# RWKV-6 attention with a hypermixer behind it on one core: both chunks' queries on partition halves, paired mix products, one exp for the chunk decays, and a new split of the copies

## The chip, the core and the metric

The kernel runs on one core of a Trainium2 chip. The metric is device time in microseconds (us). The time before is a median of 3 runs. The profile is of one further execution, taken by the hardware profiler. Engines are named as in the profile: PE (matrix products), ACT (ScalarE), DVE (VectorE), POOL (GpSimd) and SP, which only issues loads here.

## What is computed

The first part is a linear attention with a decay for each channel, over 4 batches, 8 heads, 768 steps and 48 channels a head. The second part mixes the steps of a batch with a matrix that is made from the first part's output x.

```python
for t in range(S):                                   # attention, state is D x D per head
    cur = np.einsum('bhd,bhe->bhde', u[None] * kt, vt)
    y[:, :, t] = np.einsum('bhd,bhde->bhe', rt, state + cur)
    state = wt[:, :, :, None] * state + np.einsum('bhd,bhe->bhde', kt, vt)
...
wq = x @ w_q                                         # hypermixer, x is [B, S, 384]
wk = x @ w_k
W_tok = scale * np.einsum('bsd,btd->bst', wq, wk)
mixed = np.einsum('bst,btd->bsd', W_tok, x)
return (np.maximum(mixed, 0.0) @ w_out).astype(np.float32)
```

## The kernel before

**Tiles.** A tile `n` is 256 steps of one batch, all 8 heads: 12 tiles, 3 for each batch `b`. Each tile holds two chunks of 128 steps, and a chunk lies on one half of the 128 partitions, with two steps on each partition. The steps run on different engines and are pipelined over about three tiles.

For one tile, in order: `load` brings w, k, r and v (SP issues the four transfers, into three buffers for each); `log` (ACT) takes the logarithm of w; `sums` (PE) makes its running sums in three PSUM tiles `cw0` to `cw2`, and in spare columns of `cw2` the sum over each chunk; `expk` and `expr` (ACT) turn them into the factors for k (`em`) and r (in place); `decay` (ACT) makes the decay of each chunk, `pt`, in two exps over 48 partitions each, since two heads lie one above the other with a gap; `rdec` (DVE) and `kdec` (POOL) multiply into `RdS` and `KdS`; `trR` (PE) transposes both into `psT` and `evT` (DVE) copies that to `RKT`; `amat` (PE) makes two halves of the score matrix `A` and `mask` (DVE) masks them into `AmB`; `uk1`, `uk2` (POOL), `red` (DVE) and `vd` (POOL) make the diagonal term; `vcast` (ACT) casts v; `state` and `stadd` (PE) build the chunk state `Sn`, `stev` (DVE) scales it by `pt` into `SB`; `ymat`, `yst`, `yd` (PE) sum the output `Y`, and `yev` copies it to `X`, on ACT or DVE by the table `XA`.

Then the mixer's share of the tile: `xtr` (PE) transposes X, `xev` (ACT) copies that to `XT`, `qkmat` (PE) makes wk and the transposed wq of the tile, and `qkev` (ACT) copies them in two instructions to `wk_s` and `wqT`. When all three tiles of a batch are there: `tmat` (PE) sums wk^T X over the six chunks into `Tps` (64 rows), `tev` copies it (ACT), `mix` (PE) makes six pieces of 384 columns, `mixev` (ACT) applies the maximum with 0, `fin` (PE) multiplies by w_out, `finev` copies to `osb` (ACT or DVE by the table `FE`), and `store` issues two transfers from ACT's queue.

**What sets the order.** Every engine runs its instructions strictly in the order in which the program gives them. That order is written by hand: the lists `steps`, `first`, `last`, `bsteps`, `blast` give each step a time relative to its tile or batch, `start`, `bstart`, `lstart` place the tiles, batches and loads, and all steps are sorted by the sum. The times serve as sort keys alone. PSUM is shared by two groups of buffers: two large ones, through which `psT`, the two `A`, `Sn` and `Y` pass in turn, and four of one bank (`cw0` to `cw2`, `xt_ps`, `qk`, `Tps`, `mps`, `fps`). A transfer counts on one of eight completion semaphores (DMAHW0 to 7, loads and stores alike), and waits until the transfer before it on that semaphore has landed.

Lines that the prediction speaks of: all matmuls are issued in L60; `decay` L177, X L330 (ACT) and L332 (DVE), `XT` L347, qk copies L367 and L368, `mixT` L393, `osb` L410 (ACT) and L412 (DVE), stores L417, loads L138.

Of the kernel before, what the change touches and what calls it, by code (L numbers as in the profile page):

```python
# [25 lines left out]
def kernel(  # L26
# [17 lines left out]
    XA = (0, 1, 4, 5, 7, 8, 10, 11, )  # L44
    FE = (0, 1, 1, 1, 1, 1, 0, 1, 1, 1, 1, 1, 0, 1, 0, 1, 0, 0, 0, 1, 0, 0, 0, 0)
# [29 lines left out]
    Q2 = consts.tile([C, 2], BF16, tag="Q2")  # L75
# [70 lines left out]
    def sums(n):  # L146
# [3 lines left out]
        for i, m0, m1 in ((1, BI, BS), (2, BI, BI), (0, BS, BS)):  # L150
# [122 lines left out]
    def stadd(n, q):  # L273
        T["stadd", n, q] = True
        b, m = divmod(n, NU)
        if 2 * m + q:
            SB = T["SB", b, 2 * m + q]
            mm(T["Sn", n][:, q, 0:DM], ID128, SB, start=False)

    def stev(n, q):  # L280
# [6 lines left out]
            _rep(T["pt", n][:, q], 2, D), ALU.mult)  # L287
# [32 lines left out]
    def yev(n):  # L320
# [23 lines left out]
    def xev(n):  # L344
        T["xev", n] = True
        b, m = divmod(n, NU)
        nc.scalar.copy(T["XT", b][:, :, ds(m * C2, C2)], T["tp", n])  # L347

    def qkmat(n):
# [3 lines left out]
        qk = mtile([128, 3, 2, DH], F32, "qk")  # L353
        for cc in range(2):
            for kt in range(NK):
                mm(qk[:, 0, cc], XT[:, kt, ds((2 * m + cc) * C, C)], wk_sb[:, kt],
                   start=(cc == 0 and kt == 0), stop=(kt == NK - 1))
        for kt in range(NK):
            mm(qk[0:DH, 1:3].rearrange("p a c h -> p (a c h)"), T["wq"][:, kt],
               XT[:, kt, ds(m * C2, C2)], start=False, stop=(kt == NK - 1))  # L360
        T["qk", n] = qk

    def qkev(n):
        T["qkev", n] = True
# [25 lines left out]
    def mixev(b, i):  # L390
        T["mixev", b, i] = True
        n, dt = divmod(i, NK)
        nc.scalar.activation(T["mixT", b][:, dt, ds(n * 384, 384)], T["mps", b, i],  # L393
                             ACT.Relu)
# [9 lines left out]
    def finev(b, c):  # L404
# [4 lines left out]
        if FE[b * NCH + c]:  # L409
            nc.scalar.copy(osb, T["fps", b, c])  # L410
        else:
            nc.vector.tensor_copy(osb, T["fps", b, c])  # L412
# [40 lines left out]
    for i in range(NB):  # L453
# [4 lines left out]
        nc.vector.memset(PT[i], 0.0)  # L458
# [9 lines left out]
    def wcast():  # L468
# [26 lines left out]
        (10.87, mask, (1, )),
        (11.75, state, ()),
        (12.04, stadd, (0, )),
        (12.07, stev, (0, )),
        (13.75, stadd, (1, )),
        (13.78, stev, (1, )),  # L500
        (14.31, ymat, ()),
        (14.34, yst, ()),
        (14.34, yd, ()),
        (14.37, yev, ()),
        (16.62, xtr, ()),
        (16.65, xev, ()),
        (19.39, qkmat, ()),
        (20.61, qkev, ()),
    ]
    first = [  # L510
        (-8.58, log, ()),
        (-5.99, sums, ()),
        (-1.73, expk, ()),
        (-1.72, expr, ()),
        (1.28, uk1, ()),
        (1.84, decay, ()),
        (2.87, rdec, ()),
        (4.73, trR, (0, )),
        (5.68, kdec, ()),
        (5.83, trR, (1, )),  # L520
        (5.86, evT, ()),
        (5.9, uk2, ()),
        (7.74, vcast, ()),
        (8.69, amat, (1, )),
        (9.57, amat, (0, )),
        (9.6, mask, (0, )),
        (11.89, mask, (1, )),
        (11.99, state, ()),
        (13.95, red, ()),
        (14.96, ymat, ()),  # L530
        (15.18, stadd, (0, )),
        (15.21, stev, (0, )),
        (15.57, vd, ()),
        (16.02, yd, ()),
        (16.21, stadd, (1, )),
        (16.36, stev, (1, )),
        (16.63, yst, ()),
        (16.66, yev, ()),
        (17.25, xtr, ()),
        (17.45, xev, ()),  # L540
        (20.49, qkmat, ()),
        (20.85, qkev, ()),
    ]
# [145 lines left out]
```

## Time and profile before

| | |
|---|---|
| median of 3 runs | 130.83 us (129.42 to 132.07) |
| the profiled execution | 130.25 us, its span in the profile 128.4 us |
| busy PE, DVE, ACT, POOL | 102.0, 86.6, 88.4, 85.0 us of the span |
| granted TensorE clock, mean | 0.968 of full speed |
| moved by DMA | 24.83 MB, mean 193 GB/s |

A profile row gives a start or a group, then busy time, engine, line, operation and the tiles that it writes and reads (out<-in). "[1.20 <-DVE AmB]" behind a row means that the engine stood idle 1.20 us before it, until DVE's instruction on AmB was done. The chain that ended last is followed back from the last instruction, at each step to whatever released it. PE's matmuls overlap one another: each row's time runs from the first start to the last modelled end.

### The profile page before, as it was taken

The numbers are of one execution on the slowest core, as the hardware profiler recorded it, in microseconds if no ns is written. First come the engines' busy times: TensorE is split into PE (matmuls) and PEld (weight loads), VectorE is DVE, ScalarE is ACT, GpSimd is POOL, SyncE is SP. The second block draws the span as 40 slices with busy tenths as digits, with TensorE's granted clock in tenths as the row PEclk, the third lists the DMA queues.
The fourth block names the chain that finished last, engine by engine and source line by source line (L and its number), as shares of the span: only waits on it lengthen the run. The fifth ranks groups of instructions, "written<-read, shape, count | busy, mean of one in ns | idle before, by whom it ended". The sixth has DMA issues, their size and how long they took to land.

```text
span 128.4 us, 4125 instructions
## 1 busy us (share of the span) xinstructions
PE 102.0 (79%) x1732; PEld 66.6 (52%) x1732; DVE 86.6 (67%) x134; ACT 88.4 (69%) x185; POOL 85.0 (66%) x81
## 2 busy tenths in 40 slices
PE   0076839779794999989999989799999899986900
PEld 0025437465572765645757655467566665652500
DVE  6003599788779759966959798569778979340330
ACT  3066683998885466799889686999896738456500
POOL 8859999999989759598298632999944904000000
PEclk9999976999999599999999999999999999999997
DMA  3999999999999999958025799990317300048084
GB/s 43 254 292 321 317 314 337 271 281 288 245 298 264 308 282 301 299 156 230 20 58 122 162 329 234 319 259 9 70 57 163 85 5 0 19 126 227 0 213 155
DMA packets 54738, 24.83 MB, mean 193 GB/s; under 512 B 51136, under 2 KB 54720, under 8 KB 54720
## 3 DMA queue, kind: packets, MB, share of 16 engines
q1 hardware_dynamic: 51264, 19.86, 58.2%
q10 hardware_dynamic: 3456, 4.72, 14.3%
q8 instruction: 13, 0.21, 0.6%
q14 instruction: 5, 0.04, 0.1%
HBM read 19.86 MB, written 4.72 MB: 191 GB/s over the span
## 4 chain that ended last, share of the span: by engine, by line
PE 42%; ACT 27%; DMA 11%; DVE 8%; issue 4%; ACTq 3%; DVEq 0%; SPq 0%
DMA wG<-in_w_dram 9%; PE cw L60 8%; PE psT L60 8%; PE qk L60 6%; ACT cw L170 6%; PE fps L60 5%; PE Sn L60 4%; PE Y L60 4%; ACT X L330 4%; ACT XT L347 4%; ACT em L163 4%; ACTq L417 3%; DVE RdS L186 3%; DVE AmB L230 3%; PE xt_ps L60 2%
## 5 line engine op out<-in xcount | busy, mean ns | idle before, releaser
L230 DVE TENSOR_TENSOR AmB<-A,MASK 128x1024 bf16<-128x1024 f32 x24 | 28.8, 1219 | 4.0 <-PE A L60 3.8
L236 POOL TENSOR_TENSOR uk<-kG,ubc 128x768 f32<-128x768 f32 x12 | 21.7, 1813 | 6.2 <-DMA kG<-in_k_dram 6.2
L257 POOL TENSOR_TENSOR Vd<-V,diag 128x768 bf16<-128x768 bf16 x12 | 17.7, 1473 | 9.6 <-DVE diag L250 9.1
L193 POOL TENSOR_TENSOR KdS<-kG,em 128x768 bf16<-128x768 f32 x12 | 19.7, 1638 | 6.2 <-ACT em L163 6.1
L243 POOL TENSOR_TENSOR uk<-uk,rG 128x768 f32<-128x768 f32 x12 | 21.8, 1813 | 0.6
L163 ACT ACTIVATE em<-cw,bias 128x384 bf16<-128x384 f32 x24 | 12.9, 578 | 11.2 <-PE cw L60 9.8
L186 DVE TENSOR_TENSOR RdS<-rG,cw 128x384 bf16<-128x384 f32 x24 | 12.2, 550 | 10.4 <-ACT cw L170 10.4
L60 PE MATMUL cw<-logw,BI 128*128 128x384 bf16 x36 | 11.1, 365 | 7.5 <-ACT logw L143 7.5
L284 DVE TENSOR_TENSOR SB<-Sn,pt 128x384 bf16<-128x384 f32 x20 | 11.1, 553 | 7.6 <-PE Sn L60 7.5
L213 DVE COPY RKT<-psT 128x2048 bf16<-128x2048 bf16 x12 | 14.6, 1217 | 2.1 <-PE psT L60 2.1
L60 PEld LDWEIGHTS <-KdS 64*128 64x128 bf16 (+1 forms) x256 | 12.1, 103 | 6.9 <-issue 4.0
L60 PE MATMUL fps<-wout_sb,mixT 128*128 128x384 bf16 x72 | 14.4, 327 | 0.1
L143 ACT ACTIVATE logw<-wG 128x768 bf16<-128x768 f32 x12 | 10.1, 839 | 5.9 <-DMA wG<-in_w_dram 5.9
L60 PEld LDWEIGHTS <-RKT 48*64 48x64 bf16 (+1 forms) x464 | 10.0, 104 | 7.5 <-issue 3.1
L170 ACT ACTIVATE cw<-cw,bias 128x384 f32<-128x384 f32 x24 | 12.3, 555 | 0.1
L347 ACT COPY XT<-xt_ps 128x768 bf16<-128x768 bf16 x12 | 9.6, 800 | 3.2 <-PE xt_ps L60 3.1
L412 DVE COPY osb<-fps 128x384 f32<-128x384 f32 x11 | 5.8, 553 | 8.8 <-ACT mixT L393 5.0
L250 DVE TENSOR_REDUCE diag<-uk 128x16 f32<-128x768 f32 x12 | 11.2, 944 | 0.0
L393 ACT ACTIVATE mixT<-mps 128x384 bf16<-128x384 f32 x24 | 10.6, 498 | 0.4 <-PE mps L60 0.4
L60 PE MATMUL cw<-logw,BS 128*128 128x384 bf16 x36 | 10.7, 352 | 0.0
L60 PE MATMUL A<-RKT 48*64 48x128 bf16 x384 | 9.8, 222 | 0.5 <-DVE SB L284 0.5
L60 PE MATMUL psT<-ID,RdS 128*128 128x128 bf16 x96 | 8.8, 241 | 1.8 <-DVE RdS L186 1.4
(65 smaller groups left out, 173.9 us busy)
## 6 DMA issues: line engine op xcount, KB each, us to landing
wG<-in_w_dram SPq DMA_DIRECT2D x12, 384.0 KB, 5.0
kG<-in_k_dram SPq DMA_DIRECT2D x12, 384.0 KB, 5.5
rG<-in_r_dram SPq DMA_DIRECT2D x12, 384.0 KB, 5.6
vG<-in_v_dram SPq DMA_DIRECT2D x12, 384.0 KB, 5.0
out_dram<-osb ACTq DMA_DIRECT2D x24, 192.0 KB, 2.8
wout_f<-in_moe_w_out_dram SPq DMA_DIRECT2D x1, 576.0 KB, 5.6
ubc<-in_u_dram SPq DMA_DIRECT2D x1, 192.0 KB, 4.3
wq_f<-in_moe_w_q_dram SPq DMA_DIRECT2D x1, 96.0 KB, 4.2
```

The source lines that it names most:

```text
L60: nc.tensor.matmul(o, l, rr, start=start, stop=stop, skip_group_check=True, is_transpose=trans)
L163: nc.scalar.activation(em[:, j], T["cw", n, 1 + j][:, 0:DM], ACT.Exp, bias=bias[2 + j], scale=-1.0)
L170: nc.scalar.activation(cw, cw, ACT.Exp, bias=bias[j], scale=1.0)
L186: nc.vector.tensor_tensor(pad(Rd)[:, j], jhd(T["r", n])[:, j], T["cw", n, j][:, 0:DM].rearrange("p (h d) -> p h d", d=D), ALU.mult)
L193: nc.gpsimd.tensor_tensor(pad(T["Kd", n]), jhd(T["k", n]), hd(T["em", n]), ALU.mult)
L213: nc.vector.tensor_copy(RKT, T["psT", n])
L230: nc.vector.tensor_tensor(T["AmB", n][:, js].rearrange("p q h t -> p h q t"), T["A", n, js], _rep(_rep(MASK[:, js], 1, NP), 1, 2), ALU.mult)
L236: nc.gpsimd.tensor_tensor(uk, T["k", n].rearrange("p h (j d) -> p h j d", j=2), _rep(ubc.rearrange("p (h d) -> p h d", d=D), 2, 2), ALU.mult)
L243: nc.gpsimd.tensor_tensor(uk, uk, T["r", n].rearrange("p h (j d) -> p h j d", j=2), ALU.mult)
L250: nc.vector.tensor_reduce(diag.rearrange("p j h -> p h j"), T["uk", n], axis=AX.X, op=ALU.add)
L257: nc.gpsimd.tensor_tensor(Vd, T["V2", n], _rep(T["diag", n], 3, D), ALU.mult)
L347: nc.scalar.copy(T["XT", b][:, :, ds(m * C2, C2)], T["tp", n])
```

## The change

- `decay`: the chunk sums are made with four columns for each pair of heads instead of two, and one further product with a constant (`NEG`, -100 where a head doesn't lie on that partition half) makes the exp zero there. One exp over 128 partitions and 16 columns then gives `pt`, which now has a rotating buffer instead of four zeroed ones.
- `stadd`: one product of 384 columns becomes two, each on 64 output partitions with the 192 columns of the heads that lie there.
- `qkmat`: the transposed wq of the tile's two chunks is put on the two partition halves (six products of 128 columns in place of three of 256), so that wk and wq fill one block of 128 x 256 and `qkev` copies it in one instruction to `qks`.
- `tmat`: the sum is made twice, for both partition halves. `mix` then takes a pair of products at a time, chunk 0 from the lower and chunk 1 from the upper half, into two banks.
- The copies out of PSUM are split by tables: X (`EX`), XT (`ET`), qks (`EQ`), mixT (`EM`) and osb (`EF`), 1 for ACT and 0 for DVE.
- All lists of times are new, those of the loads too.

```diff
-    XA = (0, 1, 4, 5, 7, 8, 10, 11, )
-    FE = (0, 1, 1, 1, 1, 1, 0, 1, 1, 1, 1, 1, 0, 1, 0, 1, 0, 0, 0, 1, 0, 0, 0, 0)
+    EX = (1, 1, 1, 1, 1, 1, 0, 1, 1, 1, 1, 0)
+    ET = (1, 1, 1, 0, 1, 0, 1, 1, 0, 0, 1, 0)
+    EQ = (1, 1, 1, 1, 1, 0, 1, 0, 1, 1, 0, 0)
+    EM = (1, 1, 1, 0, 1, 0, 1, 1, 1, 0, 1, 1, 1, 1, 1, 0, 1, 1, 0, 1, 1, 1, 0, 1)
+    EF = (0, 1, 1, 1, 1, 1, 1, 1, 1, 0, 1, 1, 1, 1, 1, 1, 0, 1, 1, 1, 0, 0, 0, 0)
...
-                        mm(cw[:, ds(DM + 2 * hp, 2)], lw[:, j, hp], Q2, start=False)
+                        mm(cw[:, ds(DM + 4 * hp, 4)], lw[:, j, hp],
+                           Q4.rearrange("p h c -> p (h c)"), start=False)
+                mm(cw[:, ds(DM, 4 * NP)], ID128, NEG.rearrange("p q h c -> p (q h c)"),
+                   start=False)
...
     def decay(n):
-        cw = T["cw", n, 2]
-        pt = T["pt", n] = PT[n % NB]
-        for hh in range(2):
-            nc.scalar.activation(
-                pt.rearrange("p c (q h) -> p q c h", h=2)[ds(hh * 64, D), :, :, hh],
-                cw[ds(hh * 64, D), ds(DM, 2 * NP)].rearrange("p (q c) -> p q c", c=2),
-                ACT.Exp, bias=bias_c[ds(hh * 64, D)], scale=1.0)
+        pt = hw.tile([C, H, 2], F32, name="pt", tag="pt")
+        nc.scalar.activation(pt.rearrange("p h c -> p (h c)"),
+                             T["cw", n, 2][:, ds(DM, 4 * NP)], ACT.Exp, bias=bias_c,
+                             scale=1.0)
+        T["pt", n] = pt
...
-            mm(T["Sn", n][:, q, 0:DM], ID128, SB, start=False)
+            for hh in range(2):
+                mm(T["Sn", n][ds(hh * 64, 64), q, 0:DM].rearrange(
+                    "p (q h d) -> p q h d", h=2, d=D)[:, :, hh],
+                   ID128[:, ds(hh * 64, 64)],
+                   SB.rearrange("p (q h d) -> p q h d", h=2, d=D)[:, :, hh], start=False)
...
-        nc.scalar.copy(T["XT", b][:, :, ds(m * C2, C2)], T["tp", n])
+        copy(ET[n], T["XT", b][:, :, ds(m * C2, C2)], T["tp", n])
...
         for kt in range(NK):
-            mm(qk[0:DH, 1:3].rearrange("p a c h -> p (a c h)"), T["wq"][:, kt],
-               XT[:, kt, ds(m * C2, C2)], start=False, stop=(kt == NK - 1))
-        T["qk", n] = qk
+            for q in range(2):
+                mm(qk[ds(q * DH, DH), 2:4].rearrange("p c h -> p (c h)"), T["wq"][:, kt],
+                   XT[:, kt, ds((2 * m + q) * C, C)], start=False)
+        T["qkp", n] = qk
...
-        nc.scalar.copy(T["wk", b][:, ds(2 * m, 2)], qk[:, 0])
-        nc.scalar.copy(T["wqT", b][:, ds(m * C2, C2)],
-                       qk[0:DH, 1:3].rearrange("p a c h -> p (a c h)"))
+        copy(EQ[n], T["qk", b][:, m], T["qkp", n])
...
         for c in range(NCH):
-            mm(Tps, T["wk", b][:, c], T["X", b][:, c], start=(c == 0), stop=(c == NCH - 1))
+            for q in range(2):
+                mm(Tps[ds(q * DH, DH)], T["qk", b][:, c // 2, c % 2], T["X", b][:, c],
+                   start=(c == 0), stop=(c == NCH - 1))
...
-    def mix(b, i):
-        n, dt = divmod(i, NK)
-        mps = mtile([128, 384], F32, "mps")
-        mm(mps, T["Tsb", b][:, ds(dt * 128, 128)], T["wqT", b][:, ds(n * 384, 384)])
-        T["mps", b, i] = mps
+    def mix(b, dt):
+        for q in range(2):
+            mps = T["mps", b, dt, q] = mtile([128, NU * C], F32, "mps")
+            mm(mps, T["Tsb", b][ds(q * DH, DH), ds(dt * 128, 128)],
+               T["qk", b][ds(q * DH, DH), :, 2:4].rearrange("p m c h -> p m (c h)"))
...
-    lstart = [-100, -99, -98, -9.67, 2.04, 7.29, 12.8, 20.41, 30.06, 43.64, 41.99, 60.06]
+    lstart = [-100, -99, -98, 0.02, 5.76, 12.52, 19.58, 22.33, 51.6, 58.19, 19.73, 59.04]
```

The order on the engines is shown at three places. First ACT, from tile 6's exponentials (`em`, `cw` in place) to the copy of tile 4's transposed output. Before:

```order
L163 ACTIVATE em_1217<-cw1_1200,bias2_68 128x384
L163 ACTIVATE em_1217<-cw2_1203,bias3_69 128x384
L170 ACTIVATE cw0_1214<-cw0_1214,bias0_66 128x384
L170 ACTIVATE cw1_1200<-cw1_1200,bias1_67 128x384
L177 ACTIVATE pt2_82<-cw2_1203,bias_c_70 48x4x2 x2
L330 CAST X_1049<-Y_1224 128x768
L393 ACTIVATE mixT_1064<-mps_1270 128x384
L393 ACTIVATE mixT_1064<-mps_1196 128x384
L347 COPY XT_1050<-xt_ps_1295 128x3x256
```

and after the change:

```order
L173 ACTIVATE em_1226<-cw1_1208,bias2_69 128x384
L173 ACTIVATE em_1226<-cw2_1211,bias3_70 128x384
L180 ACTIVATE cw0_1223<-cw0_1223,bias0_67 128x384
L180 ACTIVATE cw1_1208<-cw1_1208,bias1_68 128x384
L125 CAST X_1059<-Y_1231 128x768
L405 ACTIVATE mixT_1132<-mps_1297 128x384
L186 ACTIVATE pt_1304<-cw2_1211,bias_c_71 128x16
L125 COPY XT_1060<-xt_ps_1308 128x3x256
```

`pt` has moved from ahead of the copy of X to behind it and is one instruction.

Second DVE, around the scaling of r of tile 5 (`RdS`) and the two masks of tile 4 behind it. Before:

```order
L332 CAST X_1049<-Y_1008 128x768
L186 TENSOR_TENSOR RdS1_76<-rG_286,cw0_998 128x8x48
L186 TENSOR_TENSOR RdS1_76<-rG_286,cw1_984 128x8x48
L230 TENSOR_TENSOR AmB_1100<-A_1075,MASK_58 128x2x4x128
L230 TENSOR_TENSOR AmB_1100<-A_1102,MASK_58 128x2x4x128
```

and after the change:

```order
L195 TENSOR_TENSOR RdS1_76<-rG_366,cw0_1010 128x8x48
L195 TENSOR_TENSOR RdS1_76<-rG_366,cw1_995 128x8x48
L239 TENSOR_TENSOR AmB_1093<-A_1065,MASK_58 128x2x4x128
L125 COPY XT_1060<-xt_ps_1086 128x3x256
L239 TENSOR_TENSOR AmB_1093<-A_1096,MASK_58 128x2x4x128
```

The copy of X (tile 3) is gone from ahead of `RdS`, and the copy of the same tile's XT now stands between the two masks.

Third SP, the loads behind those of tile 8 (before) and of tile 7 (after), with the semaphores that each waits for. Before, the four of tile 10 and the first of tile 9:

```order
L138 DMA wG_1067<-in_w_dram 128x8x96 [waits DMAHW5_49,DMAHW4_49,Activation_49]
L138 DMA kG_1069<-in_k_dram 128x8x96 [waits DMAHW7_49,Pool_49]
L138 DMA rG_1071<-in_r_dram 128x8x96 [waits DMAHW6_49,DMAHW0_49,DVE_49]
L138 DMA vG_1073<-in_v_dram 128x8x96 [waits DMAHW1_49,Activation_49]
L138 DMA wG_1123<-in_w_dram 128x8x96 [waits DMAHW2_49,Activation_49]
```

and after the change, the last of tile 7, the four of tile 8 and the first two of tile 9:

```order
L145 DMA vG_626<-in_v_dram 128x8x96 [waits DMAHW0_49,Activation_49]
L145 DMA wG_1375<-in_w_dram 128x8x96 [waits DMAHW2_49]
L145 DMA kG_1377<-in_k_dram 128x8x96 [waits DMAHW4_49,Pool_49]
L145 DMA rG_1379<-in_r_dram 128x8x96 [waits DMAHW6_49,DVE_49,Pool_49]
L145 DMA vG_1381<-in_v_dram 128x8x96 [waits DMAHW7_49,DMAHW0_49,Activation_49]
L145 DMA wG_1576<-in_w_dram 128x8x96 [waits DMAHW2_49]
L145 DMA kG_1578<-in_k_dram 128x8x96 [waits DMAHW5_49,DMAHW3_49,Pool_49]
```

Before, tile 10's v shares DMAHW1 with a store of batch 0. After, tile 10's four stand ahead of tile 7's, and of the rows shown v of tile 8 (DMAHW7) and k of tile 9 (DMAHW3) share theirs with stores of batch 0.

## Rows read from the trace of the kernel before

**Rows 1.** Windows of core 0: length, then busy us of PE, PEld, DVE, ACT, POOL (instructions), PEclk.
```profile
40.00:50.00 10.00, 8.80 (x154) 6.09 (x155) 7.87 (x12) 5.78 (x13) 7.79 (x5) 0.83 1.07 288
...
20.00:110.00 90.00, 82.68 (x1522) 54.60 (x1521) 72.23 (x89) 71.69 (x152) 67.52 (x41) 0.97 0.73 192
```
**Rows 2.** Chain that ended last, one turn: start us, us, engine and tile.
```profile
82.03 0.20 ACT pt L177
...
82.53 0.81 ACT X L330
...
83.89 0.27 PE mps L60
...
85.43 0.62 PE qk L60 x9
```
**Rows 3.** Timeline of ACT: start us, us, instruction [idle before <-releaser].
```profile
29.53 1.05 ACT L163 ACTIVATE em<-cw,bias 128x384 bf16<-128x384 f32 x2 [0.54 <-PE cw L60]
...
36.60 1.05 ACT L163 ACTIVATE em<-cw,bias 128x384 bf16<-128x384 f32 x2 [0.42 <-POOL uk L243]
...
46.11 1.05 ACT L163 ACTIVATE em<-cw,bias 128x384 bf16<-128x384 f32 x2 [1.66 <-PE cw L60]
...
78.18 0.84 ACT L143 ACTIVATE logw<-wG 128x768 bf16<-128x768 f32 x1 [1.36 <-DMA wG<-in_w_dram]
...
120.98 4.05 ACTq L417 DMA_DIRECT2D out_dram<-osb  x6
```
**Rows 4.** Timeline of PE, five stretches.
```profile
41.85 0.82 PE L60 MATMUL Sn<-V,KdS 64*128 64x96 bf16 x16 [1.20 <-DVE AmB L230]
...
79.08 0.32 PE L60 MATMUL cw<-logw,BI 128*128 128x384 bf16 x1 [0.28 <-ACT logw L143]
...
81.35 0.50 PE L60 MATMUL Y<-Vd,PERM 64*128 64x384 bf16 x4
...
85.53 0.52 PE L60 MATMUL qk<-XT,wq_sb 128*64 128x256 bf16 x3
...
86.59 0.65 PE L60 MATMUL fps<-wout_sb,mixT 128*128 128x384 bf16 x3
87.08 0.61 PE L60 MATMUL psT<-ID,RdS 128*128 128x128 bf16 x8
...
88.83 0.48 PE L60 MATMUL cw<-logw,BS 128*128 128x384 bf16 x2
89.25 0.57 PE L60 MATMUL Y<-V,AmB 64*128 64x48 bf16 x32
...
90.20 0.50 PE L60 MATMUL Y<-Vd,PERM 64*128 64x384 bf16 x4
...
91.22 0.42 PE L60 MATMUL A<-RKT 48*64 48x128 bf16 x16
...
93.44 0.51 PE L60 MATMUL Sn<-V,KdS 64*128 64x96 bf16 x16
```
**Rows 5.** Timeline of DVE near 39 us.
```profile
38.78 0.96 DVE L332 CAST X<-Y 128x768 bf16<-128x768 f32 x1 [0.91 <-PE Y L60]
```
**Rows 6.** Groups by line and form: busy us, mean ns of one.
```profile
L213 DVE COPY RKT<-psT 128x2048 bf16<-128x2048 bf16 x12 | 14.6, 1217 | 2.1 <-PE psT L60 2.1
...
L412 DVE COPY osb<-fps 128x384 f32<-128x384 f32 x11 | 5.8, 553 | 8.8 <-ACT mixT L393 5.0 <-PE fps L60 3.8
```
**Rows 7.** Waits of SP's queue: us in total, times, longest.
```profile
SPq L138 <- DMA out_dram<-osb: 13.2, 1, 13.2
```
**Rows 8.** Chain that ended last, from the last Y to Tsb.
```profile
112.05 1.48 PE fps L60 x9
...
116.26 0.62 ACTq L417
...
116.92 0.48 ACT Tsb L381
```
**Rows 9.** Waits of all engines: us in total, times, longest.
```profile
DVE SB L284 <- PE Sn L60: 7.5, 11, 1.1
```

More of the change, by code (lines that the diff above doesn't have):

```diff
@@ L390, in mixev @@
[L390 to L394, printed above, removed]
+        T["mixT", b] = msb.tile([128, NK, 2, NU * C], BF16, name="mixT", tag="mixT")
+    def mix(b, dt):
[3 more added lines that the diff above has]
+               T["qk", b][ds(q * DH, DH), :, 2:4].rearrange("p m c h -> p m (c h)"))
@@ L408, in finev @@
         osb = T["osb", b, c // 2][:, c % 2]
[L409 to L412, printed above, removed]
+        copy(EF[b * NCH + c], osb, T["fps", b, c])
     def store(b, g):
@@ L495 @@
[L495 to L508, printed above, removed]
+        (-3.91, log, ()),
+        (-3.03, uk1, ()),
+        (-0.42, sums, ()),
+        (-0.39, expk, ()),
@@ new lines @@
+        (-0.39, expr, ()),
+        (-0.02, kdec, ()),
+        (0.09, uk2, ()),
+        (1.44, rdec, ()),
+        (1.54, decay, ()),
+        (6.05, trR, (1, )),
+        (6.21, vcast, ()),
+        (6.37, red, ()),
+        (6.46, trR, (0, )),
+        (6.82, evT, ()),
+        (7.89, amat, (0, )),
+        (9.57, mask, (0, )),
+        (9.99, amat, (1, )),
+        (10.61, mask, (1, )),
+        (10.77, vd, ()),
+        (11.56, state, ()),
+        (11.59, stadd, (0, )),
+        (13.28, stev, (0, )),
@@ L509 @@
+        (14.31, stadd, (1, )),
+        (14.34, stev, (1, )),
+        (14.88, ymat, ()),
+        (14.96, yd, ()),
+        (15.01, yst, ()),
+        (15.04, yev, ()),
+        (17.24, xtr, ()),
+        (17.46, xev, ()),
+        (20.52, qkmat, ()),
+        (21.16, qkev, ()),
     ]
     first = [
[L511 to L518, printed above, removed]
@@ L537 @@
[L537 to L542, printed above, removed]
+        (-0.64, log, ()),
+        (-0.1, uk1, ()),
+        (3.13, sums, ()),
+        (3.16, expk, ()),
+        (4.25, expr, ()),
+        (4.55, kdec, ()),
+        (4.58, trR, (1, )),
+        (5.39, decay, ()),
+        (5.42, rdec, ()),
+        (6.03, trR, (0, )),
+        (6.12, vcast, ()),
+        (7.21, uk2, ()),
+        (7.68, evT, ()),
@@ new lines @@
+        (8.49, amat, (0, )),
+        (9.75, amat, (1, )),
+        (11.19, mask, (0, )),
+        (11.22, mask, (1, )),
+        (13.4, red, ()),
+        (13.93, vd, ()),
+        (14.27, state, ()),
+        (15.2, stadd, (0, )),
+        (15.64, stev, (0, )),
+        (15.67, stadd, (1, )),
+        (15.81, ymat, ()),
+        (15.84, yst, ()),
+        (15.92, stev, (1, )),
+        (15.93, yd, ()),
+        (15.96, yev, ()),
+        (17.78, xtr, ()),
+        (18.79, xev, ()),
+        (21.33, qkmat, ()),
@@ L562 @@
[L562 to L576 removed]
+        (-9.8, uk1, ()),
+        (-5.81, log, ()),
+        (-0.72, sums, ()),
@@ new lines @@
+        (-0.17, expk, ()),
+        (-0.17, expr, ()),
+        (-0.14, rdec, ()),
+        (1.08, decay, ()),
+        (2.37, kdec, ()),
+        (3.03, uk2, ()),
+        (5.28, vcast, ()),
+        (5.61, trR, (1, )),
+        (7.18, trR, (0, )),
+        (7.21, evT, ()),
+        (9.13, red, ()),
+        (9.46, amat, (0, )),
+        (12.13, amat, (1, )),
+        (12.53, state, ()),
+        (13.0, mask, (0, )),
+        (13.03, mask, (1, )),
+        (14.03, stadd, (0, )),
+        (14.93, stev, (0, )),
@@ L577 @@
+        (15.53, vd, ()),
+        (16.58, ymat, ()),
+        (16.61, yst, ()),
+        (16.78, yd, ()),
+        (20.84, yev, ()),
+        (20.87, xtr, ()),
+        (22.06, xev, ()),
+        (22.94, qkmat, ()),
+        (23.25, qkev, ()),
+        (28.8, stadd, (1, )),
+        (28.83, stev, (1, )),
     ]
```

236 lines of the change are left out of this document (84 added, 152 removed).

## The prediction

> **What bounds the kernel now.** I read the busy time of the middle first. Between 20 and 110 us, where eleven of the twelve tiles pass, DVE and ACT are each busy for about 72 of 90 us, POOL for 67.5 and PE for 82.7 [rows 1] (a PE that counts as busy isn't full, since its matmuls are pipelined). Four engines that are loaded to three or four fifths and still stop one another mean a loop of waits, so the chain that ended last is the view that counts. Part of one turn of it stands in [rows 2]: ACT makes the exponentials of a tile, then the two small exps of the decays (pt), then copies the finished output X of a tile two places earlier; PE transposes X, and everything queued behind that (a product of the mixer, qk, state, transposes, and at last cw, the running sums of a later tile) must pass before ACT can start the next tile's exponentials. ACT's starts of em for tiles 3, 4 and 5 [rows 3] give the length of a turn: 36.60 - 29.53 = 7.07 us, but 46.11 - 36.60 = 9.51 us. The end is another regime: behind the last Y the work is one chain [rows 8] with little beside it, and then come six store issues in a row on ACT's queue.
>
> The profiled execution took 130.25 us (span 128.4 and 1.85 around it), inside the runs of 129.42 to 132.07 and 0.6 below their median. The sum is made against 130.25.
>
> **Part by part.**
>
> *Decays.* Two exps on 48 partitions become one on 128, and it moves behind the copy of X (the ACT place shown above). In the chain X starts 0.50 after pt began [rows 2], and six turns have pt in the chain. It doesn't bring 0.5 each, because X also needs Y: in that turn Y's last products end at 81.35 + 0.50 = 81.85 [rows 4] and X starts at 82.53, so 0.68 is to be had; in the other five the same difference is 0.30 to 0.40. Together 2.3, less 0.05 a time for the signal: **-2.0**. The single exp then stands in ACT's wait for the transposes of X; were that wait gone, it would cost about half of the pair, 0.25 a tile. The running sums get one more matmul, 16 columns wide. By the rate of A below 16 columns are under 0.01, and it has a weight load of its own; I take 0.03 in each of some ten turns: **+0.3**.
>
> *X on ACT for tiles 2, 3 and 9.* On DVE the copy stands ahead of the next tile's RdS. For tile 2 it holds DVE 0.96 from 38.78 [rows 5]; RdS and AmB come late, PE stands idle 1.20, and its next 16 Sn matmuls take 0.82 where they take 0.51 at 93.44 [rows 4]. [...] This is the turn of 9.51; against 7.07 it has 2.4 too much. I take 2.3 for tile 2, nothing for tile 3 (another product holds PE there) and 0.4 for tile 9: **-2.7**.
>
> *qk.* Three products of 256 columns on one half of the array's columns become six of 128 that alternate between the halves. Three in 0.52 [rows 4] are 3 x 0.11 and a tail of 0.17 in which the result runs out. That parts of the array overlap is shown by A: 16 matmuls of 128 columns on four quarters take 0.42, that is four rounds of 0.053 and a tail, not sixteen. So 0.16 less, eight times in the chain ahead of the end: **-1.3**.
>
> *Mix.* Six single products a batch, K = 64, become three pairs on the two row halves. Y<-Vd shows such pairs: four of 384 columns in 0.50, two rounds of 0.16 and the tail [rows 4]. A single one costs the chain 0.27 [rows 2], eight times; four pairs at 0.33 instead: **-0.85**. tmat doubles to twelve, in pairs on column halves: nothing if they overlap as A's do, 0.96 a batch (six rounds of 0.16) if not.
>
> *stadd.* One product of 384 columns over the full array becomes two of 192 on column halves: 0.08 less if they overlap. But it leaves the full array. Where the next group has the same shape it starts 0.16 ahead of the end of the last (fps ends at 87.24, psT starts at 87.08), where the shape changes 0.06 (cw ends at 89.31, Y<-V starts at 89.25) [rows 4]. So a change costs 0.10, and each stadd adds one or two: net +0.07 on average, nine times in the chain: **+0.6**. [...]
>
> *DVE takes XT of tiles 3, 5, 8, 9, qks of 5, 7, 10 and four mixT* ahead of the last batch, and gives up three osb. DVE copies 384 float columns in 0.55 and 2048 bf16 ones in 1.22 [rows 6], from which I estimate 0.55 for XT (768 bf16) and 0.42 for qks (256 float). In full: 4 x 0.55 + 3 x 0.42 + 4 x 0.55 - 3 x 0.55 = +4.0. But XT stands between two AmB (the DVE place shown above) while PE makes the second A, so 0.15 of each shows, 0.6; qks stands ahead of diag and shows in full, 1.3; mixT stands ahead of a RdS that mostly waits for ACT, half, 1.1; the osb give back half, 0.8. **+2.2**. ACT is rid of these eleven and of the second exp and the second qk copy of each tile; but waits, not its load, set the turn, so nothing is counted for that beyond the terms above. If its load did set it, the gain is larger.
>
> *Loads.* One of tile 10's loads waited 13.2 us on SP for a store [rows 7], with which it shares a completion semaphore, and tile 9's w stood behind it in the queue. In the new order tile 10's loads are issued ahead of tile 7's, and those that now share a semaphore with a store (v of tile 8 and k of tile 9, the SP place above) have about a turn of slack. What the stall cost: PE waited for tile 9's log 0.28 [rows 4], ACT for its w 1.36 [rows 3]: **-0.5**, nearer PE, which the chain goes back to. Tile 10 then holds one of three buffers for long, so that tiles 7 to 9 load into two: their loads start behind the reads of the tile two places before, still about a turn ahead of use.
>
> *End.* From the end of the last Y (112.05) to the start of Tsb (116.92) are 4.87 [rows 8]: three fps ahead of the transposes, XT, qk, and 0.62 behind a store's issue. Now one fps is left there: X on DVE 0.96, transposes 0.5, XT 0.55, qk 0.65, qks 0.42, the rest of tmat 0.5, signals 0.3: 3.9. **-1.0**. Behind it nothing: the six mixT are shared out, but the last six store issues take 4.05 in a row as before [rows 3].
>
> *Sum:* -2.0 + 0.3 - 2.7 - 1.3 - 0.85 + 0.6 + 2.2 - 0.5 - 1.0 = -5.25; 130.25 - 5.25 = **125.0**.
>
> **Rivals.** (a) The forecast, 122.5 to 127.6. (b) DVE's additions are absorbed (2.2) and the stall counts as ACT saw it (0.9 more): -8.35, 121.9. For it: DVE idles 17.8 of the 90 us. (c) The shortened loop only hands over to another, POOL's 67.5 us of work or DVE's strict order: half of the savings of 8.35 arrive, the costs of 3.1 stay: -1.1, 129.2. (d) Column halves with all rows in use don't overlap, which A, with part of the rows, doesn't prove: qk's 1.3 is lost, stadd costs 0.7 more, and tmat up to 3.8, of which half is charged: 125.0 + 3.9 = 128.9. [...] (e) Slower: DVE works strictly in its order, and each of the eleven moved instructions and the three osb left to it waits for its own product of PE, with AmB, SB and RKT queued behind. If each wait is as long as SB's for Sn, 7.5 over 11 times = 0.68 [rows 9], that is +9.5, and the additions in full +1.8 more: 136. It decides, slower than 132.9, from a mean wait of about 0.45. Against it: PE issues these products ahead of those that the queued work needs.
>
> **Numbers.** Chances: (a) 0.60, (b) 0.14, (c) 0.10, (d) 0.07, (e) 0.09. Two per cent, 2.6 us, is about what a measurement of this kernel can tell from no change. a and b are faster, less a little of a's upper edge: 0.73; c, d and that edge: 0.18; e: 0.09. The range reaches from a little under b to a little over c, 121.0 to 129.6, and leaves out e and the far tails. The likeliest case's own range is the 122.5 to 127.6 above.
>
> **What would show it.** X right behind the exponentials on ACT, no pt ahead of it in the chain; no turn over 9 us near 40 and no drop of the clock there; qk's second group at about 0.36; two mps in 0.33; no long wait of SP for a store before the end; Tsb some 4 us behind the last Y. It would be wrong with waits of half a microsecond ahead of XT, qks or mixT on DVE and AmB late behind them, with Tps at 2 us, with a turn still over 8 us, or with ACT waiting for the loads of tiles 7 to 9.

## The result and the profile after

The changed kernel takes **125.88 us** (median of 4 runs, 125.75 to 126.07); the kernel before, run beside it, 130.94 (129.42 to 132.07). The ratio is 0.9652, with a 95% interval of 0.9569 to 0.9736: faster by 3.5%. The profiled execution of after took 125.75, its span 123.6, 4.8 less than before's. A second set of runs gave 126.22 (125.19 to 126.37) and the same ratio. Ratios and their intervals leave out runs that took over 1.5% longer than the fastest of the same kernel.

The middle first, as in [rows 1] (length, then busy us of PE, PEld, DVE, ACT, POOL, the granted clock, DMA share, GB/s):

```profile
40.00:50.00 10.00, 9.19 (x205) 6.32 (x205) 9.34 (x13) 7.21 (x14) 9.69 (x7) 1.00 1.12 261
20.00:110.00 90.00, 84.12 (x1675) 55.76 (x1673) 76.61 (x102) 66.30 (x129) 70.09 (x43) 0.98 0.87 208
```

ACT is rid of 5.4 us, DVE has 4.4 more, and the clock no longer falls between 40 and 50: it is 1.00 there, where [rows 1] have 0.83. In windows of 1 us the granted clock of before is 0.50 from 42 to 45, behind the 1.20 us in which PE stood idle, and 1.00 from 46 to 50. The order on ACT, against [rows 3] (timeline of ACT: start us, us, instruction, idle before it and what ended that):

```profile
30.21 1.05 ACT L173 ACTIVATE em<-cw,bias 128x384 bf16<-128x384 f32 x2
...
37.08 1.06 ACT L173 ACTIVATE em<-cw,bias 128x384 bf16<-128x384 f32 x2 [0.58 <-PE cw L64]
...
39.17 0.80 ACT L125 CAST X<-Y 128x768 bf16<-128x768 f32 x1
39.87 0.28 ACT L186 ACTIVATE pt<-cw,bias_c 128x16 f32<-128x16 f32 x1
...
44.00 1.06 ACT L173 ACTIVATE em<-cw,bias 128x384 bf16<-128x384 f32 x2 [0.79 <-PE cw L64]
...
58.98 0.84 ACT L150 ACTIVATE logw<-wG 128x768 bf16<-128x768 f32 x1 [2.47 <-DMA wG<-in_w_dram]
...
61.69 0.58 ACT L173 ACTIVATE em<-cw,bias 128x384 bf16<-128x384 f32 x1
```

The three em at the top are tiles 3, 4 and 5: turns of 6.87 and 6.92 us, where [rows 3] have 7.07 and 9.51. The log at 58.98 is that of tile 7, and it waits 2.47 us for its load; the turn from tile 6 to 7 is the longest now, 9.47. The turn from tile 5 to 6 has stayed at 8.22, and those from 8 to 11 take 8.25, 8.01 and 8.05. The starts of em in both traces cut the span into stretches:

| stretch | before | after | difference |
|---|---|---|---|
| start to em of tile 3 | 29.53 | 30.21 | +0.68 |
| tile 3 to 5 | 16.58 | 13.79 | -2.79 |
| tile 5 to 7 | 16.85 | 17.69 | +0.84 |
| tile 7 to 11 | 34.10 | 31.94 | -2.16 |
| tile 11 to the span's end | 31.34 | 29.97 | -1.37 |

The chain that ended last, which in [rows 2] passed from ACT to PE and back in each turn, now stays on PE from 80.51 to the last Y, over 27 us. Part of it (start us, us, engine and tile):

```profile
80.51 0.51 PE xt_ps L64 x6
...
84.15 1.00 PE psT L64 x16
85.15 1.20 PE cw L64 x15
86.35 0.49 PE fps L64 x3
86.84 1.28 PE Y L64 x44
88.12 0.35 PE A L64 x16
```

PE's new shapes (timeline of PE, against [rows 4]):

```profile
79.90 0.34 PE L64 MATMUL mps<-qks,Tsb 64*128 64x384 bf16 x2
...
82.34 0.27 PE L64 MATMUL Sn<-SB,ID 128*64 128x192 bf16 x2
...
83.80 0.36 PE L64 MATMUL qk<-XT,wq_sb 128*64 128x128 bf16 x6
...
95.31 1.17 PE L64 MATMUL Tps<-X,qks 128*64 128x384 bf16 x12
```

And the waits of all engines (us in total, times, longest), where [rows 9] had 7.5 over 11 for SB:

```profile
ACT logw L150 <- DMA wG<-in_w_dram: 10.8, 5, 4.5
...
DVE mixT L407 <- PE mps L64: 1.9, 2, 1.7
DVE qks L125 <- PE qk L64: 1.7, 2, 1.0
...
DVE SB L297 <- PE Sn L64: 1.3, 2, 0.9
```

The end, against [rows 8] (the chain again):

```profile
107.00 1.40 PE Y L64 x44
...
108.43 0.97 DVE X L125
...
112.33 0.49 ACT Tsb L392
```

Tsb starts at 112.33, and Y's last products end at 108.39: 3.94, where it was 4.87.

### The profile page after: what moved, and what is told of

Its sections match the earlier page's. It is cut to its first block, busy times and chain, and to the rows that moved or that the text cites. A ratio compares the mean times of both kernels' runs of the same rounds, so it can differ in the third digit from the quotient of the medians.

```text
span 123.6 us, 4278 instructions
## 1 busy us (share of the span) xinstructions
PE 98.2 (79%) x1820; PEld 64.0 (52%) x1820; DVE 89.3 (72%) x142; ACT 79.5 (64%) x152; POOL 84.8 (69%) x81
## 2 busy tenths in 40 slices
DMA packets 54739, 24.85 MB, mean 201 GB/s; under 512 B 51136, under 2 KB 54720, under 8 KB 54720
## 5 line engine op out<-in xcount | busy, mean ns | idle before, releaser
L64 PEld LDWEIGHTS <-KdS 64*128 64x128 bf16 (+1 forms) x256 | 10.9, 97 | 8.7 <-POOL KdS L202 2.9
L64 PE MATMUL cw<-logw,BS 128*128 128x384 bf16 x36 | 11.2, 369 | 0.0
L125 ACT COPY osb<-fps 128x384 f32<-128x384 f32 x17 | 8.0, 486 | 3.7 <-PE fps L64 3.6
L64 PE MATMUL psT<-ID,KdS 128*128 128x128 bf16 x96 | 8.1, 232 | 2.8 <-POOL KdS L202 1.9
L206 ACT CAST V<-vG 128x768 bf16<-128x768 f32 x12 | 10.0, 836 | 0.0
L125 ACT CAST X<-Y 128x768 bf16<-128x768 f32 x10 | 8.1, 805 | 3.0 <-PE Y L64 2.5
```

Source lines behind the costliest of these rows:

```text
L64: nc.tensor.matmul(o, l, rr, start=start, stop=stop, skip_group_check=True, is_transpose=trans)
L125: (nc.scalar.copy if e else nc.vector.tensor_copy)(o, i)
```

## The experiments

All are timed beside the kernel before. "The changed kernel" is 125.88 and 126.22, its two medians.

**The changed kernel again.**

> The changed kernel once more, unaltered, as the anchor for the kernels run beside it. It should give 125.9 us, as in its first runs (125.75 to 126.07), and show whether the transfers of 10 to 50 us move about 260 GB/s again, as in its first trace, or about 300, as in the trace of before.

126.22 us, and 262 GB/s between 10 and 20 us as in its first trace. So the slower transfers belong to this kernel and not to the occasion.

**The place of the decays, undone in the changed kernel.**

```diff
-        (1.54, decay, ()),
+        (-0.385, decay, ()),
```

> The changed kernel with the one exp for the decays moved back behind the four other exps and ahead of X of the tile before, where before had its two. Theory (the exp's place was worth time, as the prediction priced it): X starts 0.28 us later in each turn, and what follows it too, eleven turns at 0.1 to 0.28 us, so 127 to 129 us. Rival (X is no longer what TensorE waits for, since the chain of waits of the changed kernel runs over TensorE nearly all through): within 0.4 us of the anchor.

125.38 us (125.24 to 126.23), ratio 0.9619 (0.9582 to 0.9655): not slower, and by the medians 0.5 to 0.8 faster, though the interval overlaps that of the changed kernel (0.9610 to 0.9695). The theory is out: in the changed kernel the place of the exp is worth nothing.

**The place of the decays alone, in the kernel before.**

```diff
-        (-1.0, decay, ()),
+        (0.8, decay, ()),
```

> The kernel before with its two exps for the decays moved behind X of the tile before, and nothing else changed. Theory (the prediction priced the exp and its place at 2.0 us, nearly all of it the place): 128.6 us, and no pt in the chain of waits. Rival (as the changed kernel with the exp moved early showed, the place is worth nothing since X is not what is waited for longest): within 0.7 us of before.

132.31 us (131.59 to 132.97), ratio 1.0167 (1.0076 to 1.0259): slower than before, which neither side expected. From em to em, four turns are shorter by 0.26 to 0.32 us (tile 3 to 4: 7.07 to 6.81; 6 to 7: 8.63 to 8.37; 9 to 10 and 10 to 11 likewise). In these X starts 0.26 to 0.58 sooner behind em, so the gain at X is there. But the turn of tile 2 to 3 grows from 8.11 to 8.69, 7 to 8 from 9.10 to 9.95, and 8 to 9 from 8.02 to 8.49. Only the second of these is shown to be the exp's doing. The timeline of ACT there:

```profile
65.76 1.76 ACTq L417 DMA_DIRECT2D out_dram<-osb  x2
67.56 0.56 ACT L177 ACTIVATE pt<-cw,bias_c 48x8 f32<-48x8 f32 x2 [1.09 <-issue]
```

and the chain that ended last:

```profile
66.50 1.02 ACTq L417
...
67.84 0.28 ACT pt L177
...
68.17 0.65 PE fps L60 x3
```

X starts 0.27 sooner here too, but pt falls behind two store issues that hold ACT for 1.76, and PE's fps waits for pt. By the program, pt reads the last of cw2 and so holds one of the four PSUM banks that fps needs.

In the turn of tile 2 to 3, XT starts 5.45 behind em, where before has 4.89. ACT in this run, then in before:

```profile
21.65 0.58 ACT L163 ACTIVATE em<-cw,bias 128x384 bf16<-128x384 f32 x1 [2.65 <-PE cw L60]
...
27.10 0.80 ACT L347 COPY XT<-xt_ps 128x768 bf16<-128x768 bf16 x1
```

```profile
21.42 1.10 ACT L163 ACTIVATE em<-cw,bias 128x384 bf16<-128x384 f32 x2 [2.65 <-PE cw L60]
...
26.31 0.79 ACT L347 COPY XT<-xt_ps 128x768 bf16<-128x768 bf16 x1
```

That looks like the length of pt, but isn't. The run below that moves only copies of X later in the program has pt in its old place, and in this turn XT 5.40 behind em and a length of 8.62:

```profile
21.83 0.58 ACT L163 ACTIVATE em<-cw,bias 128x384 bf16<-128x384 f32 x1 [2.65 <-PE cw L60]
...
27.23 0.79 ACT L347 COPY XT<-xt_ps 128x768 bf16<-128x768 bf16 x1
```

So this turn differs by half a microsecond between executions with pt ahead of X. The turn of tile 8 to 9 ends with the log of tile 9, which waits 1.86 for w in place of 1.36 [rows 3]: w is issued at 74.71 instead of 71.91, both times behind a load that waits for a store. Whether the exp's place causes that isn't shown.

**X of tiles 2, 3 and 9, undone in the changed kernel.**

```diff
-    EX = (1, 1, 1, 1, 1, 1, 0, 1, 1, 1, 1, 0)
+    EX = (1, 1, 0, 0, 1, 1, 0, 1, 1, 0, 1, 0)
```

> The changed kernel with X of tiles 2, 3 and 9 copied by VectorE again, as before the change. Theory (this move took the turn of tile 2 from 9.51 to 6.92 us): +2.3 to +2.7 us, so about 128.4 us, with the long turn of over 9 us near 36 to 46 us back and the clock under 0.9 in the window 40 to 50. Rival (that turn was long because X stood on VectorE behind the decays, the reduce and the masks of another order, and the new order removes it anyway): within 0.6 us of the anchor, no turn longer there than 7.5 us.

127.07 us (126.40 to 127.82), ratio 0.9718 (0.9664 to 0.9771): 0.9 to 1.2 slower by the medians. The intervals of the ratios overlap a little, but no run is as fast as any of the eight of the changed kernel. Window and timeline of ACT in the profiled execution:

```profile
40.00:50.00 10.00, 7.75 (x145) 5.49 (x145) 7.90 (x12) 5.67 (x10) 7.18 (x6) 0.83 1.14 257
```

```profile
37.23 1.06 ACT L173 ACTIVATE em<-cw,bias 128x384 bf16<-128x384 f32 x2 [0.58 <-PE cw L64]
...
46.64 0.58 ACT L173 ACTIVATE em<-cw,bias 128x384 bf16<-128x384 f32 x1 [1.82 <-PE cw L64]
...
59.50 0.85 ACT L150 ACTIVATE logw<-wG 128x768 bf16<-128x768 f32 x1
```

The long turn is back, 37.23 to 46.64 = 9.41 us, and so is the clock at 0.83. So the mechanism is that of the theory. But the total pays less than the 2.5 us of that turn: the log of tile 7 no longer waits for its load, since everything else is late, and the turn of tile 6 to 7 takes 8.36 instead of 9.47. The loads had eaten part of the gain.

**The same move alone, in the kernel before.**

```diff
-    XA = (0, 1, 4, 5, 7, 8, 10, 11, )
+    XA = (0, 1, 2, 3, 4, 5, 7, 8, 9, 10, 11, )
```

> The kernel before with X of tiles 2, 3 and 9 copied by ScalarE and nothing else changed. Theory (the prediction priced this move at 2.7 us, 2.3 of them at tile 2): about 128 us, the turn after em at 36.60 near 7 us in place of 9.51 and no clock drop in the window 40 to 50. Rival (that turn is long for the order around it): within 0.8 us of before.

128.44 us (128.00 to 131.37), ratio 0.9879 (0.9841 to 0.9918): 1.2% or 1.6 us faster. Timeline of ACT and window:

```profile
37.53 1.05 ACT L163 ACTIVATE em<-cw,bias 128x384 bf16<-128x384 f32 x2 [0.42 <-PE cw L60]
...
44.67 1.05 ACT L163 ACTIVATE em<-cw,bias 128x384 bf16<-128x384 f32 x2 [0.48 <-PE cw L60]
```

```profile
40.00:50.00 10.00, 8.97 (x177) 6.00 (x173) 8.33 (x11) 8.56 (x16) 9.84 (x7) 1.00 1.05 278
```

The turn is 7.14 long, 2.4 shorter, and the clock is 1.00 from 40 to 50. Of the 2.7 forecast, about 1.6 arrive at the end. In the profiled execution tile 3 starts 0.92 later than in that of before, ahead of any copy that was moved, so where the rest goes can't be read from it.

**Queries on one half again, single products.** The old qkmat, qkev, tmat and mix in the changed kernel's order; its core:

```diff
-            for q in range(2):
-                mm(Tps[ds(q * DH, DH)], T["qk", b][:, c // 2, c % 2], T["X", b][:, c],
+            mm(Tps, T["wk", b][:, c], T["X", b][:, c], start=(c == 0), stop=(c == NCH - 1))
...
-            mm(mps, T["Tsb", b][ds(q * DH, DH), ds(dt * 128, 128)],
+            mm(mps, T["Tsb", b][:, ds(dt * 128, 128)], T["wqT", b][:, ds(q * 384, 384)])
```

> The changed kernel with the queries of all chunks on partitions 0 to 63 again: qk's second group is three products of 256 columns, Tps six products, the products of mix share their rows and so follow one another, and qks is copied by two instructions, on the engine that had the one. Theory (the prediction's terms: 1.3 for qk, 0.85 for mix): TensorE busy about 2 us more (98.2 to 100.3) and the time +2.1 us against the anchor, about 128.1 us, a little more for the second copy. Rival (TensorE waits in these places anyway): TensorE's busy time rises, but the time stays within 0.6 us of the anchor.

127.27 us (126.92 to 127.77), ratio 0.9784 (0.9706 to 0.9862): 1.1 to 1.4 slower. PE is busy 100.5 us in place of 98.2, as told. From its timeline of PE:

```profile
84.00 0.52 PE L64 MATMUL qk<-XT,wq_sb 128*64 128x256 bf16 x3
...
112.40 1.14 PE L64 MATMUL Tps<-X,wk_s 128*64 128x384 bf16 x6
```

qk's group is 0.16 longer than the 0.36 above, as forecast. Six products of Tps on one column half take 1.14, twelve on both took 1.17: column halves with all 128 rows in use do run side by side. About half of PE's saving of 2.3 reaches the total.

**XT, qks and mixT back on ACT** (tiles 3 to 10, batches 0 to 2):

```diff
-    ET = (1, 1, 1, 0, 1, 0, 1, 1, 0, 0, 1, 0)
-    EQ = (1, 1, 1, 1, 1, 0, 1, 0, 1, 1, 0, 0)
+    ET = (1, 1, 1, 1, 1, 1, 1, 1, 1, 1, 1, 0)
+    EQ = (1, 1, 1, 1, 1, 1, 1, 1, 1, 1, 1, 0)
...
```

> The changed kernel with XT, qks and mixT of tiles 3 to 10 copied by ScalarE again (batch 3 and tile 11 left as they are), so that VectorE gives up about eight copies (3 XT at 0.55, 3 qks at 0.42, 2 or more mixT at 0.55 us). Theory (the prediction's sum, where these copies on VectorE cost 2.2 us together because VectorE waits in order): 0.5 to 2 us faster than the anchor. Rival (they sat in VectorE's idle time, and ScalarE, given them back, delays X and the exps): the same within 0.6, or slower.

127.66 us, but with runs from 126.08 to 129.31, ratio 0.9737 (0.9605 to 0.9868) against 0.9652 (0.9610 to 0.9695) for the changed kernel. A gain of the 2.2 us that the prediction charged lies outside what these runs allow; one of up to about 0.7 doesn't. The edit moves eleven copies, more than the eight told: all that the prediction charged. And the run shows only a net. From 20 to 110 us, against the second trace of the changed kernel, DVE is rid of 5.4 us (77.0 to 71.6 busy) and ACT has 4.6 more (66.5 to 71.1). So moving these copies to DVE was no loss of 2.2; what they cost there, and what ACT gains by being rid of them, isn't told apart.

**Loads in the order of the tiles.** First what the changed kernel does (timeline of SP's queue; the first row is w of tile 10, the last w of tile 7):

```profile
45.95 1.35 SPq L145 DMA_DIRECT2D wG<-in_w_dram  x1
...
52.28 1.27 SPq L145 DMA_DIRECT2D wG<-in_w_dram  x1
```

```diff
-    lstart = [-100, -99, -98, 0.02, 5.76, 12.52, 19.58, 22.33, 51.6, 58.19, 19.73, 59.04]
+    lstart = [-100, -99, -98, 0.02, 5.76, 12.52, 19.58, 22.33, 51.6, 54, 58.19, 59.04]
```

> The changed kernel with its loads issued in the order of the tiles, 9 and 10 behind 8, in place of the four loads of tile 10 standing ahead of those of tiles 7 to 9. Theory (the stall seen in the changed kernel's trace, ScalarE waiting 2.47 us for w of tile 7 and GpSimd 2.25 us for its k, lengthens the turn from tile 6 to 7 to 9.47 us): that wait is gone, that turn comes to about 7.7 us, and the time falls by 1 to 2 us to 124 to 125 us. Rival (as the prediction's text had it, the loads stand a turn ahead and cost nothing, or the time that is won there is lost again behind the next late load, of tile 10): within 0.5 us of the anchor.

124.64 us (124.54 to 124.82), ratio 0.9550 (0.9530 to 0.9569): 1.2 to 1.6 faster than the changed kernel. The log of tile 7 starts at 56.72 with no wait (timeline of ACT), and its turn is 8.35 in place of 9.21 in the run beside it:

```profile
56.72 0.85 ACT L150 ACTIVATE logw<-wG 128x768 bf16<-128x768 f32 x1
```

**Where the load buffers begin.** The two rows of SP above show a second thing: an issue takes SP 1.35 and 1.27 us there, and from 38 to 60 us all but two take 1.25 to 1.45. And the transfers move 261 GB/s from 10 to 20 us, where those of the kernel before move 318 (windows, before and after):

```profile
10.00:20.00 10.00, 6.38 (x89) 4.88 (x90) 6.71 (x9) 6.67 (x14) 9.92 (x7) 0.89 1.17 318
```

```profile
10.00:20.00 10.00, 5.89 (x85) 4.35 (x86) 5.97 (x8) 6.46 (x12) 7.57 (x5) 0.99 1.26 261
```

From 10 to 40 us, the stretch that the texts below name, it is 262 against 296. All kernels made from the changed one shared the lower rate, all made from before the higher. In the program's layout the buffers begin at byte 54144 of a partition before and at 53920 after: NEG, 32 bytes, is new, and four small tiles are gone. 54144 is a multiple of 128, 53920 lies 32 above one. Three runs move them. NEG at 64 bytes (53952, 64 above a multiple):

```diff
-    NEG = consts.tile([C, NP, 2, 2], BF16, tag="NEG")
+    NEGP = consts.tile([C, 2 * NP, 2, 2], BF16, tag="NEG")
+    NEG = NEGP[:, 0:NP]
```

> The changed kernel with the tile NEG made 64 bytes long per partition in place of 32 (only its first half is used), and nothing else changed. In the kernel before, the buffers of the loads begin at multiples of 64 bytes; the 32 bytes of NEG, new in the change, put all of them at 32 above one. Theory (that offset is why the changed kernel moves 260 GB/s from 10 to 40 us where before moved 317): 300 GB/s or more there, w landing in 5 us in place of 6.2 to 6.6, the start of tile 3 about 0.7 us earlier, the wait for w of tile 7 (2.2 to 2.5 us) shorter by at least 1, and the time 0.7 to 1.7 us below the changed kernel's 125.9 to 126.2. Rival (the rate is set by something else that the change did, such as the time of the issues): 260 GB/s again and the same time.

```profile
10.00:20.00 10.00, 5.55 (x84) 4.05 (x85) 6.02 (x8) 6.46 (x12) 7.67 (x5) 0.94 1.28 262
```

125.70 us (124.81 to 126.02), ratio 0.9608 (0.9533 to 0.9684): as the rival said, no change of rate. The kernel before, moved up by 32 (Q2's tile at 64 bytes):

```diff
-    Q2 = consts.tile([C, 2], BF16, tag="Q2")
+    Q2P = consts.tile([C, 32], BF16, tag="Q2")
+    Q2 = Q2P[:, 0:2]
```

> The kernel before with its tile Q2 made 64 bytes long in place of 32 (4 are used), so that the buffers of its loads begin 32 bytes above a multiple of 64, as in the changed kernel. Theory (the offset sets the rate): about 260 GB/s from 10 to 40 us in place of 317, tile 3 starting about 0.7 us later, and 0.7 to 2 us slower than before. Rival: 300 GB/s or more as before and the same time within 0.5.

```profile
10.00:20.00 10.00, 6.07 (x83) 4.21 (x84) 6.01 (x8) 7.00 (x14) 8.60 (x6) 0.97 1.27 263
```

263 GB/s, 132.50 us (130.79 to 134.08), and a ratio to before of 1.0122 (1.0071 to 1.0173): the shift alone costs the kernel before 1.6 us. It moves every tile behind Q2 by 32, so the time needn't all be that of the loads. But the place does set their rate, and 64 isn't the grid. The last run tests 128; the run ahead of it is the same kernel with 64.

**A version that beats both.** The changed kernel with NEG at 64 bytes, loads in order, and every second store of the last batch on SP's queue:

```diff
-            nc.scalar.dma_start(
+            (nc.sync if b == B - 1 and j else nc.scalar).dma_start(
```

> The changed kernel with three things together: NEG at 64 bytes, the loads in the order of the tiles as in the run that measured 124.6, and every second store of the last batch issued by SyncE in place of ScalarE. Theory: 124.6, less 0.7 for the faster loads at the start, less 1.3 for the end (the last two of six issues in a row on ScalarE, 0.68 us each, run beside one another, and the four ahead of them are no longer in their way): 122.6 us. Rival for the end (the landing of the last store ends the span, whoever issues it): no gain there, about 123.9.

124.30 us (124.06 to 124.49), ratio 0.9511 (0.9464 to 0.9558), with 263 GB/s from 10 to 20 us. The end gave little: from the last Y (107.25) to the span's end (122.2) are 14.95, where after has 15.2. Its windows at the end say why (the last two columns, DMA share and GB/s):

```profile
117.00:118.00 1.00, 0.00 (x0) 0.00 (x0) 0.00 (x1) 0.00 (x0) 0.00 (x0) 1.00 0.97 281
118.00:119.00 1.00, 0.00 (x0) 0.00 (x0) 0.00 (x0) 0.00 (x0) 0.00 (x0) 1.00 0.97 223
```

The DMA share is 0.97 here and 0.98 in the next microsecond. The six stores of 192 KB are issued from 115.0 to 117.0, where after has 116.1 to 119.4, but they take longer to land: 2.9 to 4.1 us from issue to landing, 3.7 in the median, against 2.8 to 3.3 and 3.1 in after. With NEG at 128 bytes (buffers from 54016, a multiple of 128):

> The kernel of the run before, with loads in the order of the tiles and stores on two queues, and with NEG now 128 bytes long, so that the load buffers begin at multiples of 128 bytes, as they do in the kernel before, and no longer at 64 above one. Theory (a run of 384 bytes wants to begin on a multiple of 128; this explains both why 32 more slowed the kernel before to 260 GB/s and why 64 did not help the changed one): 300 GB/s or more from 10 to 40 us, no waits of 1.4 to 1.6 us for w of tiles 1 and 2, tile 3 starting at 29.4 in place of 30.03, and 0.4 to 1 us less than 124.3. Rival (the rate hangs on another difference, such as the order in which the first loads are issued in the changed kernel): 260 GB/s and 124.3 again.

```profile
10.00:20.00 10.00, 6.30 (x90) 4.71 (x91) 6.34 (x9) 6.24 (x12) 8.63 (x6) 0.98 1.14 310
```

310 GB/s; w of tile 1 is waited for 0.73 instead of 1.52, and w of tile 2 not at all instead of 1.40. Tile 3 starts at 29.61 instead of 30.03. (By itself that proves little: in two runs of the kernel before, with its buffers in place and 320 GB/s or more, tile 3 starts at 30.34 and 30.45.) The time is **123.90 us** (123.52 to 124.00), ratio 0.9496 (0.9452 to 0.9540). That is the best of all runs, 2 us below the changed kernel with no change to its arithmetic. The step from 64 to 128 bytes is 0.4 us by the medians, and no run of either kernel reaches into the other's; by the ratios it is 0.2, which is less than their intervals.

## Why the prediction was right, and where it was not

The time, 125.88 against 125.0, lies in forecast (a)'s own range. Its parts agree less well.

| step | forecast us | what the runs showed us |
|---|---|---|
| decays, place and one exp | -2.0 | place: 0 in the changed kernel, +1.7% alone in before |
| NEG's product | +0.3 | no run; 0.01 to 0.02 a turn in the chain |
| X on ACT | -2.7 | -1.6 alone in before; +0.9 to 1.2 when undone |
| qk and mix on halves | -2.15 | +1.1 to 1.4 when undone |
| split stadd | +0.6 | no run |
| DVE's copies | +2.2 | undoing them gains 0.7 at most |
| loads | -0.5 | order +1.2 to 1.6; buffers off the grid up to +0.4 |
| end | -1.0 | -0.93 |

*Decays.* The step that failed is the sum over six turns. X does start sooner where pt is out of its way, and four turns of the kernel before were shorter when only this was done, 1.15 together and not 2.3. In another turn the moved exp came behind two store issues, PE waited for it, and the turn was 0.85 longer. That pt holds cw2's bank until it has run was not in the working at all. In the changed kernel, where the chain runs over PE, undoing the place costs nothing. NEG's product costs about what was told or less: cw with it takes 1.20 or 1.31 in the chain, against 1.18 to 1.19 or 1.30 in the chain of before. The 0.05 a time for the signal was an estimate; from the last Y to the end the chain of after has gaps of 0.02 to 0.05 between engines.

*X on ACT.* Right in place, cause and size of the turn: 9.51 to 6.92, back to 9.41 when undone, with the clock (0.83, 1.00 and 0.83 from 40 to 50). The term was too large because 2.4 us won in one turn aren't 2.4 at the end: in the changed kernel the load of tile 7, which comes in at its own pace, takes a part back. What does so in the kernel before isn't shown.

*Halves.* Each price was met (0.36 for qk, 0.34 for a pair of mps, 1.17 for twelve Tps), so rival (d) is out: twelve products of Tps on both column halves take 1.17 us, six on one half 1.14. The steps that the prices are made of, 0.16 for 384 columns and from that 0.11 for 256 and 0.053 for 128, and the tail of 0.17, are estimates: in [rows 4] one, two and three products of 384 columns take 0.32, 0.48 and 0.65. About half of the sum came through.

*DVE's copies.* Charged 1.5 or more too dear, the largest error on that side. The prediction charged XT, qks and mixT in full or by half, as if DVE had something late behind them, and put ACT's relief at nothing. Which of the two was wrong the runs don't separate. The profile speaks for the first: it has two waits for qks, two for mixT, the longest 1.7 us and near the end, and SB's wait fell from 7.5 to 1.3 us. DVE idled where PE's products were late, and the copies seem to have gone there. Rival (e), 0.68 a time, falls with that; rival (b) was nearer in this part.

*Loads.* The stall on SP is gone, but "about a turn ahead of use" was wrong, and the prediction's last sentence names just this as a sign of failure (beside "a turn still over 8 us", which came too, in five turns behind tile 5). Tile 10's loads, put ahead of tile 7's, take one of three buffers and four issues of SP; w of tile 7 is then issued at 52.28 and waited for until 58.98. That the new constant and the tiles that went would put every buffer 32 bytes off wasn't looked at, and cost another part.

*End.* 3.94 against 3.9 forecast.

*What stays open.* The measured parts add up to about -1.6 (0 - 1.6 - 1.1 + 0 + 2.0 - 0.9), the whole to about -4.7. That sum is only a rough one: the parts come from different kernels, and the loads' part is measured against an order that the kernel before doesn't have. No run took the new order of the steps by itself, which the prediction has no term for, nor the split stadd (its pair takes 0.27, 0.20 of it in the chain). Where some of the rest shows is plain: from tile 7 to tile 11, -2.16, of which the turn 7 to 8 alone gives 9.10 - 7.63 = 1.47; this turn stays at 7.38 to 7.57 in the runs that undo the decays' place, X, the halves and the copies. So what made it short is what those runs keep, most likely the order; that is argued, not shown. That 125.0 was so near is luck as much as pricing: savings put too high by some 4 us and loads that lose about 2 met a cost put too high and gains that had no term.

## What to carry to other kernels

A stall that is taken off a chain is worth what the next releaser leaves over: for an instruction that is moved and not removed, write down what stands behind its new place before giving it a gain. Ask of each load when its buffer comes free and what stands ahead of it in the issuing queue, again after every change of the order. When a tile is added or resized, look at where the transfer buffers begin: here a shift by 32 bytes cost the kernel before 1.6 us.

## What was not expected of the hardware

Loads in runs of 384 bytes move 310 to 321 GB/s from 10 to 20 us into buffers that begin at a multiple of 128 bytes, and 261 to 263 into buffers 32 or 64 bytes above one (five layouts, each rate seen in kernels of both orders). In the order of the kernel before, the rate at 32 is 263/318 = 0.83 of that at a multiple of 128; in that of the changed kernel it is 261/310 = 0.84 at 32 and 263/310 = 0.85 at 64. So 64 above costs as much as 32. The time from issue to landing says the same: in the median 5.0 to 5.6 us for w, k, r and v in the kernel before, 5.8 to 6.3 with its buffers 32 higher. The packets are as many and as small in both, 54738 with 51136 of them under 512 bytes. What it is in a transfer that the place slows down, no run shows, and no run has buffers 96 above a multiple of 128.
